# Gated linear attention and a squared-ReLU network on one core: later loads of q, k, v and alpha, pairs of blocks at other places, another order of the opening

## The chip, the cores and the metric

The kernel runs on one core of a Trainium2 chip. The time is that of one execution on the device, in microseconds (us); three executions were timed, and one more was profiled.

## The reference

Four batches, eight heads, 768 steps, head width 48. A state of 48x48 for each head is scaled by alpha and fed by k and v; y is q times the state. The heads of one step side by side are a row x of 384; 3072 such rows go through a network with 2048 hidden units.

```python
for t in range(S):
    state = alpha[:, :, t, :, None] * state + np.einsum('bhd,bhe->bhde', k[:, :, t], v[:, :, t])
    y[:, :, t] = np.einsum('bhd,bhde->bhe', q[:, :, t], state)
...
x = np.ascontiguousarray(attn_out.transpose(0, 2, 1, 3)).reshape(B * S, H * D)
h = np.maximum(x @ w_in, 0.0)
return (h * h @ w_out).astype(np.float32)
```

The inputs and the result stand in DRAM; q, k, v and alpha are float32. The weights arrive as eight-byte floats and are turned into float32 on the chip.

## The kernel before

**Blocks and groups.** A block is 128 steps of one batch with all eight heads; there are 24, numbered so that the four batches of the same steps follow each other. The attention works on pairs of blocks (n, n+1), the network on groups of four blocks (512 rows), six groups. While the network works on group g, the attention makes the x of group g+1, so that TensorE always has products of the network between those of the attention.

**Attention of a block.** `ln` takes the logarithm of alpha (in place, ScalarE), `cs` sums it along the steps (TensorE), `eb` and `ei` take the exponentials of the sums with both signs, `mq` and `mk` multiply q and k by them (VectorE). `qT`, `kT` (for the first blocks) or `turn` (a pair) transpose q and k on TensorE, and `qc`, `kc` copy them from PSUM (ScalarE). `sc` makes the scores, `kv` (state_sums) the sums of k times v, `am` masks the scores, `us` adds the state, `st` makes the next state. `ga` and `gb` are the two halves of a pair's products: each has scores and sums of one new block, and the products y of the pair before. `ya`, `yb` are the y of the first pairs alone. `ev`, in the opening `ep`, copies y from PSUM to x, in four parts; the table `evd` says which copies VectorE takes, the others are ScalarE's. `lt` (lastT) or `bl` and `br` (over DRAM, rows `row` and `last`) bring the last sums of a block to where the state wants them. `zeros` and `warm` are products of zeros, which nobody reads.

**The network.** In group 0 the weights are used in float32 (lines 908 and 798). They come in sixteen parts (`raw`), and each is converted by `first` (VectorE, two operations), `middle` (ScalarE, two) and `second` (VectorE, three). `ha` and `hb` are the first layer's products for the first and second half of group 0's rows, for one slice j of 128 hidden units; each is three matmuls of 256 columns. From group 1 on, and for part of w_out in group 0, each product is made of three passes on parts of the operands: `cast_w`, `rest_w` and `diff_w` split a part of the weights into b, l and d; l and d are stored to DRAM (line 652) and come back part by part (line 683). x is split into xa, xl, xd (`split_x` on ScalarE and VectorE, `diff_x` on VectorE), the hidden values into ha, hl, hd. `in_x` does the first two passes of a slice and `in_y`, two slices later, the third; `out_x` and `out_y` do the same for the second layer. The sums of the output are added on VectorE (`osb`) and stored.

**What sets the order.** The order of each engine is the order of the program. The opening is written out by hand in the string `first`. After it, `weave` goes through a list of the network's units, each with a cost in rows, and puts the attention's events, and those for weights and x, ahead of the first unit that starts at or after their time. The table `AT` holds all those times: `g0`, `g1`, `g` when a pair of blocks starts in group 0, group 1 and later groups; `ga`, `gb` when its two halves come after that; `evs`, `evs0` the distance of the four parts of `ev`; `w_first`, `o0`, `o2`, `wstep`, `w_in_at`, `w_in_by` when the parts of the weights are split; `g0x`, `g1x`, `gx`, `xs` when x is split; `cv0` when the conversions start; `str1` when d of w_out comes back.

**Loads.** All transfers are issued by SyncE, in order; an issue that waits for a buffer holds up those behind it, and each of the eight semaphores of the transfers serves every eighth of them. q, k, v and alpha of a block are four loads of 192 KB. There are two tiles for alpha and for q, three for k, four for v, and a few lent ones in the opening; so a load waits until an earlier block's tile has been read. In `attention`, the next k is asked for with `ga`, two v and one more k with `gb`, two q with `turn`, and alpha with `cs`.

**PSUM.** Eight banks go round among all tiles of TensorE's results; a tile's first product waits until its bank's previous tile was read.

Of the kernel before, what the change touches and what calls it, by code (L numbers as in the profile page):

```python
# [15 lines left out]


GB = 4
AT = {'evs': 0.65, 'lead': 4, 'post': 3, 'w_first': (44.75, 40.75, 51.5), 'wstep': 1.8, 'w_in_at': 2.375, 'w_in_by': 3.4, 'room1': 22, 'room': 24, 's0': 4, 'ahead': 6, 'late': 2, 'xs': 0.2, 'g0': ((0.75, 4, False, True, 25.5), (21.25, 6, True, True), (28.25, 8, True, False)), 'sc0': (2.15, 2.35, 2.35), 'g1': ((5.75, 8, False, 15.5), (15.25, 10, True), (34.5, 12, True)), 'g': ((1.575, 6, True), (15.5, 8, True)), 'g1x': 50.0, 'gx': 46.75, 'g0x': 56.25, 'k0': 2, 'h0': 17, 'k1': 4, 'h1': 0, 'h1by': 2, 'evs0': 0.1, 'tp': 'ADMD', 'tp1': 'ADAD', 'split': 8, 'o0': (46.5, 47.25), 'o1': (), 'o2': (19.75, 27.0, 32.75, 34.0, 42.0, 41.75), 'str1': 24.5, 'ga': 9.5, 'gb': 12.75, 'cv0': 1.125, 'pre': '0a 1a 0q 0k 1k 1q', 'cp': (), 'evd': ((0, 0, 0), (0, 1, 0), (0, 1, 2), (2, 0, 2), (2, 1, 1), (2, 1, 2), (2, 1, 3)), 'first': 'ln0 warm0 ln1 cs0 zeros3 ei0 mk0 eb0 mq0 kT0 cs1 qT0 kc0 eb1 load0v load2a qc0 mq1 sc0 ei1 ln2 qT1 mk1 weights0 qc1 kv0 am0 load1v us0 kT1 kc1 load2k lt1 sc1 kv1 first0 load2q load3a load2v am1 middle0 cs2 eb2 us1 ei2 ya0 yb0 mk2 ln3 mq2 qT2 qc2 cs3 ep00 ep01 load3v load3k ep02 kT2 weights1 kc2 zeros2 load3q second0 lt0 sc2 eb3 kv2 ei3 ep03 zeros3 first1 weights2 middle1 ha0 mq3 mk3 qT3 load4k kT3 qc3 kc3 am2 load4q ha1 second1 sc3 lt2 lt3 st0 kv3 am3 us2 ha2 us3 load4a first2 ya2 yb2 weights3 ep20 ep21 ha3 weights4 ep22 ep23 middle2 st3 hb1 load4v second2 weights5 weights6 st2 hb2 st1 hb3 hb0'}


RUN = {0: 128, 32: 32, 64: 64, 96: 32}
# [3 lines left out]
def kernel(  # L26
# [84 lines left out]
    def load(n, xs="aqkv"):  # L111
        c, b = divmod(n, B)
        for x in xs:
            t = tile_of(x, n)
            if id(t) in owner:
                need(("free", *owner[id(t)]))
            owner[id(t)] = x, n
            given.add((x, n))
            nc.sync.dma_start(  # L119
                out=t[:, :, 0:D] if x in "qk" else t.rearrange("a (h d) -> a h d", h=H),  # L120
                in_=srcs[x][b, :, c * C : (c + 1) * C, :].rearrange("h s d -> s h d"),
            )
# [73 lines left out]

    for word in AT["pre"].split():
        load(int(word[0]), word[1:])
# [53 lines left out]
    def work(name, bufs=1):  # L252
        return p2.tile([128, NP, C], FP32, tag=name, name=name, bufs=bufs)
# [7 lines left out]

    SPLIT = AT["split"]

# [98 lines left out]
    def copied(x, n):  # L362
        t = blk[n][f"{x}s"] = work(f"{x}s", 2 if x == "k" else 4)
        copy = nc.vector.tensor_copy if f"{x}{n}" in AT["cp"] else nc.scalar.copy
        copy(out=t, in_=blk[n].pop(f"{x}T"))
# [219 lines left out]
    def ev(n, ps=tuple(range(NP))):  # L585
# [44 lines left out]
    here, todo, room = {}, [], [22]  # L630
# [8 lines left out]
    late = [False]  # L639
# [20 lines left out]
    def diff_w(w, p):  # L660
# [7 lines left out]
        for x in "ld":  # L668
            t = made.pop((x, w, p))
            if w == "i" or p >= NW - AT["k0"] or (x == "l" and p >= NW - AT["k1"]):  # L670
                here[x, w, p] = t
        pump()

    def prepare(at, w, p):
        step = AT["wstep"]
        fs = (cast_w, rest_w, diff_w)
        return [(at + i * step, f, (w, p)) for i, f in enumerate(fs)]
# [288 lines left out]
    first = AT["first"]  # L966
# [28 lines left out]
    def attention(t, n0, after, scale=1, begun=True, whole_at=None, turn_at=None):  # L995

        out = []
        old = n0 - 2 if after else None
        given = old, n0 if begun and n0 < NBLK else None

        def loads(at, *which):
            out.extend((at, load, (m, x)) for m, x in which if m < NBLK)

        for at, fs in EARLY if n0 < SPLIT else PLAN:
            for f in fs.split():
                w = t + (AT[f] if scale == 1 and f in ("ga", "gb") else at) * scale
                if f in ("ga", "gb") and whole_at is not None:
                    w = whole_at
                if f in ("turn", "kc0", "kc1", "qc0", "qc1", "br0", "br1") and turn_at is not None:
                    w = turn_at + (at - 6.5) * scale  # L1010
                if f == "ga":
                    out.append((w, ga if whole_at is None else joined, given))
                elif f == "gb":
                    if whole_at is None:
                        out.append((w, gb, given))
                    if after:
                        for p in range(NP):
                            out.append((w + AT["evs" if scale == 1 else "evs0"] * p, ev_part, (old, p)))
                if not begun:
                    continue  # L1020
                if f == "ga":
                    loads(w, (n0 + 3, "k"))
                elif f == "gb":
                    loads(w, (n0 + 2, "v"), (n0 + 3, "v"), (n0 + 4, "k"))
                elif n0 >= NBLK:
                    continue
                elif f == "turn":
                    out.append((w, turn, (n0,)))
                    loads(w, (n0 + 2, "q"), (n0 + 3, "q"))
                else:  # L1030
                    n = n0 + int(f[-1])
                    out.append((w, steps[f[:-1]], (n,)))
                    if f[:-1] == "cs":
                        loads(w, (n + 2, "a"))
        return sorted(out, key=lambda x: x[0])

    def weave(units, events, at):
# [55 lines left out]
    cv0 = AT["cv0"]  # L1093
# [10 lines left out]
    for (t, n0, after, run, *other), scale in zip(AT["g0"], AT["sc0"]):  # L1104
        events += attention(t, n0, after, scale, run, *other)
    for g in range(1, NG):
        base.append(begin + sum(u[0] for u in units))
        at0 = base[g]
        units.append((0, begun, (g,)))
        units += layer_in(g) + layer_out(g)  # L1110
        units.append((0, ended, (g,)))
        if g + 1 < NG:
            for t, n0, after, *other in AT["g1"] if g == 1 else AT["g"]:
                n0 = n0 if g == 1 else n0 + GB * g
                other = [None if x is None else at0 + x for x in other]
                events += attention(at0 + t, n0, after, 1, True, *other)
            events += [(at0 + t, f, x) for t, f, x in splits_of_x(AT["g1x" if g == 1 else "gx"], g + 1)]
        if g == 1:
            m = len(AT["w_first"])
            for p in range(m, NW):  # L1120
                events += prepare(at0 + AT["w_in_at"] + AT["w_in_by"] * (p - m), "i", p)
            for i, at in enumerate(AT["o1"] + AT["o2"]):
                events += prepare(at0 + at, "o", order[len(AT["o0"]) + i])
            n = min(AT["k0"], AT["k1"])
            events.append((at0, lambda: todo.extend(("l", "o", p) for p in range(NW - n, NW)), ()))
            events.append((at0 + AT["str1"], stream_out, (AT["k1"], "d")))
        events.append((at0 + 26, stream, (g + 1,)))
# [31 lines left out]
```

## Time and profile before

| what | us |
|---|---|
| median of three runs | 525.36 |
| lowest, highest | 524.78, 529.82 |
| the profiled execution | 526.78 |
| its span, first to last instruction | 525.0 |

The granted clock was 1.000 throughout. The page gives busy time by engine (PE is TensorE's matmuls, PEld its weight loads, DVE is VectorE, ACT ScalarE, POOL GpSimd, SP SyncE), the span in 40 slices with a digit for tenths of busy time, and the chain of work that ended last. "issue" in it is time in which an engine waited for nothing that the profile shows. A wait is written as the waiting engine and line, an arrow, and what ended it, then the total in us, how often, and the longest. A row of the timeline has its start, its length, the engine, the line, the operation and in brackets the idle time before it.

TensorE's busy time is spread so: 4.9 us lie in zeros, 3.8 in warm, 43.3 in the first layer of group 0, 203 in the passes of the first layer later, and 312 in the second layer, of which 54 in float32; the rest is attention.

### The profile page before, as it was taken

What the parts mean: (1) busy time and instruction counts of PE and PEld (TensorE: products, weight loads), DVE (VectorE), ACT (ScalarE), POOL (GpSimd) and SP (SyncE); (2) the same over time, 40 slices, a digit from 0 to 9 for tenths busy, and PEclk for the clock granted to TensorE, in tenths of its full rate; (3) what the DMA queues carried; (4) which work ended last, traced back from release to release, by engine and by line L of the source; (5) the groups of instructions that cost most, each with busy time, mean ns of one, the idle gap of its engine ahead of it and who ended that gap; (6) DMA issues with size and microseconds to landing.
All of it is one profiled execution on the core that took longest, in us unless ns stands there. A gap on an engine that the chain in (4) does not pass through costs nothing.

```text
span 525.0 us, 13021 instructions
## 1 busy us (share of the span) xinstructions
PE 511.3 (97%) x5346; PEld 421.9 (80%) x5346; DVE 362.9 (69%) x627; ACT 305.2 (58%) x650; POOL 5.3 (1%) x29
## 2 busy tenths in 40 slices
PE   8879999999999999999999999999999999999997
PEld 6665455669888669887899987889987899988997
DVE  3677979989879859766596566686464486463861
ACT  5658896575779645475963166953265763164620
POOL 4000000000000000000000000000000000000000
PEclk9999999999999999999999999999999999999999
DMA  9998877555589665998995787855683444699201
GB/s 189 228 248 169 238 162 180 112 153 227 182 221 218 173 192 157 286 305 201 203 263 167 236 234 196 228 162 167 208 282 126 159 151 139 212 373 308 82 2 60
DMA packets 139323, 102.35 MB, mean 195 GB/s; under 512 B 109808, under 2 KB 112896, under 8 KB 139264
## 3 DMA queue, kind: packets, MB, share of 16 engines
q1 hardware_dynamic: 139264, 101.52, 68.6%
q8 instruction: 42, 0.69, 0.5%
q14 instruction: 17, 0.14, 0.1%
HBM read 84.17 MB, written 17.33 MB: 193 GB/s over the span
## 4 chain that ended last, share of the span: by engine, by line
PE 92%; SPq 3%; issue 1%; DMA 1%; ACT 1%; DVE 1%; DVEq 0%; POOLq 0%
PE o L798 41%; PE h L715 31%; PE h L908 7%; PE y L390 4%; SPq L119 3%; PE sckv L410 2%; PE T L567 2%; PE sckv L438 2%; DMA raw<-in_moe_w_in_dram 1%; PE cs L283 1%; PE cs L284 1%; PE cs L280 1%; SPq L136 0%; ACT hid L917 0%; PE lastT L334 0%
## 5 line engine op out<-in xcount | busy, mean ns | idle before, releaser
L715 PE MATMUL h<-xa,wb 128*128 128x512 f32 x240 | 68.8, 395 | 0.0
L715 PE MATMUL h<-xl,wl 128*128 128x512 f32 x240 | 67.8, 391 | 0.9 <-issue 0.9
L715 PE MATMUL h<-xd,wd 128*128 128x512 f32 x240 | 66.7, 393 | 0.1
L605 ACT COPY x<-y 32x256 f32<-32x256 f32 (+3 forms) x134 | 47.9, 365 | 23.2 <-PE y L390 21.0
L637 DVE TENSOR_TENSOR hid<-h,hid 128x512 f32<-128x512 f32 x40 | 27.6, 689 | 46.9 <-PE h L715 46.7
L732 ACT ACTIVATE h<-h 128x512 f32<-128x512 f32 x40 | 23.3, 582 | 62.2 <-PE h L715 62.2
L798 PE MATMUL o<-wb,ha 128*128 128x384 f32 x160 | 54.4, 340 | 1.3 <-issue 1.3
L715 PEld LDWEIGHTS h<-xl,wl 128*128 128x128 f32 x240 | 45.0, 188 | 11.0 <-issue 1.1
L798 PE MATMUL o<-wd,hd 128*128 128x384 f32 x304 | 53.8, 334 | 0.0
L798 PE MATMUL o<-w_out,hid 128*128 128x384 f32 x160 | 53.7, 490 | 0.0
L798 PE MATMUL o<-wl,hl 128*128 128x384 f32 x160 | 53.5, 335 | 0.0
L798 PEld LDWEIGHTS o<-wd,hd 128*128 128x128 f32 x304 | 52.7, 188 | 0.2
L715 PEld LDWEIGHTS h<-xd,wd 128*128 128x128 f32 x240 | 44.5, 188 | 9.7 <-issue 0.5
L715 PEld LDWEIGHTS h<-xa,wb 128*128 128x128 f32 x240 | 44.3, 188 | 9.1
L798 PE MATMUL o<-wb,hx 128*128 128x384 f32 x144 | 48.7, 338 | 0.0
L798 PE MATMUL o<-wl,hx 128*128 128x384 f32 x144 | 48.1, 334 | 0.0
L908 PE MATMUL h<-x,w_in 128*128 128x512 f32 (+1 forms) x120 | 43.3, 510 | 2.9 <-issue 2.0
L798 PEld LDWEIGHTS o<-w_out,hid 128*128 128x128 f32 x160 | 29.9, 190 | 19.9 <-ACT w_out L180 0.2
L730 ACT ACTIVATE hid<-h 128x512 f32<-128x512 f32 x40 | 24.2, 606 | 29.3 <-PE h L715 29.2
L690 ACT ACTIVATE ha<-hid 128x512 fp32r<-128x512 f32 x40 | 25.4, 637 | 25.6 <-DVE hx L642 17.2
L908 PEld LDWEIGHTS h<-x,w_in 128*128 128x128 f32 x120 | 22.3, 190 | 20.4 <-issue 16.9
L642 DVE SCALAR_TENSOR_TENSOR hl<-ha,hid 128x512 fp32r<-128x512 f32 x40 | 27.5, 686 | 12.2 <-ACT ha L690 12.2
(114 smaller groups left out, 869.4 us busy)
## 6 DMA issues: line engine op xcount, KB each, us to landing
wd<-do SPq DMA_DIRECT2D x36, 384.0 KB, 4.9
wl<-lo SPq DMA_DIRECT2D x34, 384.0 KB, 4.4
wl<-li SPq DMA_DIRECT2D x32, 384.0 KB, 4.2
wd<-di SPq DMA_DIRECT2D x32, 384.0 KB, 3.5
raw<-in_moe_w_in_dram SPq DMA_DIRECT2D x8, 768.0 KB
raw<-in_moe_w_out_dram SPq DMA_DIRECT2D x8, 768.0 KB, 4.8
v_in<-in_v_dram SPq DMA_DIRECT2D x24, 192.0 KB, 4.3
out_dram<-osb SPq DMA_DIRECT2D x24, 192.0 KB, 2.4
```

Source lines behind the costliest of these rows:

```text
L119: nc.sync.dma_start(out=t[:, :, 0:D] if x in "qk" else t.rearrange("a (h d) -> a h d", h=H), in_=srcs[x][b, :, c * C : (c + 1) * C, :].rea ...
L390: ins = nc.tensor.matmul(out=ys[e][64 * half : 64 * half + D + G * e, m % 2, p // 2, t], lhsT=lhsT, rhs=rhs, start=(half, e) not in seen, ...
L410: nc.tensor.matmul(out=ps[e][HALF[h], 0, p, :], lhsT=ks[rows, p, HALF[h]], rhs=qs[rows, p, HALF[h]], start=True, stop=True, skip_group_che ...
L605: copy(out=x[kk][to : to + m, t : t + 2], in_=blk[n]["y"][e][r : r + m, :, p // 2],)
L637: nc.vector.tensor_tensor(out=o, in0=x, in1=z, op=op)
L642: nc.vector.scalar_tensor_tensor(out=o, in0=x, scalar=c, in1=y, op0=ALU.mult, op1=op)
L690: nc.scalar.activation(out=a, in_=x, func=AF.Copy, scale=NEAR * E)
L715: nc.tensor.matmul(out=acc["h", j], lhsT=here[w, "i", p][:, kk, jj * 128 : (jj + 1) * 128], rhs=x_parts[x][:, kk], start=start and kk == 0 ...
L730: nc.scalar.activation(out=hid[j], in_=x, func=AF.Copy, scale=E)
L732: nc.scalar.activation(out=x, in_=x, func=AF.Copy, scale=1.0 + E)
L798: nc.tensor.matmul(out=acc[t][:, 0:DM], lhsT=lhs[:, t * C : (t + 1) * C], rhs=rhs, start=start, stop=stop, skip_group_check=True,)
L908: nc.tensor.matmul(out=ps, lhsT=w[:, kk, c0 : c0 + 128], rhs=xT[g][kk][:, cols], start=(kk == 0), stop=(kk == KM - 1),)
```

## The change

`attention` asks for each of its seven loads at a time of its own, by a list `later` of seven numbers, in rows: k of block n0+3 with `ga` as before, v of n0+2 with `gb` as before, v of n0+3 five rows after it, k of n0+4 four rows after it, q of n0+2 with `turn` as before, q of n0+3 one row later, alpha one row after `cs`. In group 0 (scale not 1) nothing is later.

```diff
+        later = AT["later"] if scale == 1 else (0,) * 7
...
                 if f == "ga":
-                    loads(w, (n0 + 3, "k"))
+                    loads(w + later[0], (n0 + 3, "k"))
                 elif f == "gb":
-                    loads(w, (n0 + 2, "v"), (n0 + 3, "v"), (n0 + 4, "k"))
+                    for i, m, x in ((1, n0 + 2, "v"), (2, n0 + 3, "v"), (3, n0 + 4, "k")):
+                        loads(w + later[i], (m, x))
...
                 elif f == "turn":
                     out.append((w, turn, (n0,)))
-                    loads(w, (n0 + 2, "q"), (n0 + 3, "q"))
+                    loads(w + later[4], (n0 + 2, "q"))
+                    loads(w + later[5], (n0 + 3, "q"))
...
                     if f[:-1] == "cs":
-                        loads(w, (n + 2, "a"))
+                        loads(w + later[6], (n + 2, "a"))
```

The table `AT` is one line of the file; these are the entries of it that change, one to a line:

```diff
+'later': (0, 0, 5, 4, 0, 1, 1)
-'evs': 0.65, 'evs0': 0.1
+'evs': 0.5, 'evs0': 0.5
-'w_first': (44.75, 40.75, 51.5), 'wstep': 1.8, 'w_in_at': 2.375, 'w_in_by': 3.4
+'w_first': (46.75, 40.5, 50.75), 'wstep': 1.4, 'w_in_at': 2.25, 'w_in_by': 3.6
-'xs': 0.2, 'g1x': 50.0, 'gx': 46.75, 'g0x': 56.25
+'xs': 0.05, 'g1x': 52.0, 'gx': 48.25, 'g0x': 55.75
-'g0': ((0.75, ...), (21.25, ...), (28.25, ...)), 'sc0': (2.15, 2.35, 2.35)
+'g0': ((-0.25, ...), (22.25, ...), (28.25, ...)), 'sc0': (2.45, 2.35, 2.35)
-'g1': ((5.75, 8, False, 15.5), (15.25, 10, True), (34.5, 12, True))
+'g1': ((4.5, 8, False, 16.25), (14.25, 10, True), (34.75, 12, True))
-'g': ((1.575, 6, True), (15.5, 8, True))
+'g': ((2.075, 6, True), (14.25, 8, True))
-'o0': (46.5, 47.25), 'o2': (19.75, 27.0, 32.75, 34.0, 42.0, 41.75), 'str1': 24.5
+'o0': (47.5, 46.75), 'o2': (22.0, 26.25, 25.25, 38.5, 39.75, 35.0), 'str1': 19.5
-'ga': 9.5, 'gb': 12.75, 'cv0': 1.125, 'pre': '0a 1a 0q 0k 1k 1q'
+'ga': 9.75, 'gb': 12.5, 'cv0': 0.875, 'pre': '0a 1a 0q 0k 1q 1k'
-'evd': ((0, 0, 0), (0, 1, 0), (0, 1, 2), (2, 0, 2), (2, 1, 1), (2, 1, 2), (2, 1, 3))
+'evd': ((0, 1, 0), (0, 1, 2), (2, 0, 2), (2, 1, 0), (2, 1, 1), (2, 1, 2), (2, 1, 3))
```

The opening's order (`first`), the same steps but for zeros2, which is gone:

```diff
-ln0 warm0 ln1 cs0 zeros3 ei0 mk0 eb0 mq0 kT0 cs1 qT0 kc0 eb1 load0v load2a qc0 mq1 sc0 ei1 ln2 qT1 mk1 weights0 qc1 kv0 am0 load1v us0 kT1 kc1 load2k lt1 sc1 kv1 first0 load2q load3a load2v am1 middle0 cs2 eb2 us1 ei2 ya0 yb0 mk2 ln3 mq2 qT2 qc2 cs3 ep00 ep01 load3v load3k ep02 kT2 weights1 kc2 zeros2 load3q second0 lt0 sc2 eb3 kv2 ei3 ep03 zeros3 first1 weights2 middle1 ha0 mq3 mk3 qT3 load4k kT3 qc3 kc3 am2 load4q ha1 second1 sc3 lt2 lt3 st0 kv3 am3 us2 ha2 us3 load4a first2 ya2 yb2 weights3 ep20 ep21 ha3 weights4 ep22 ep23 middle2 st3 hb1 load4v second2 weights5 weights6 st2 hb2 st1 hb3 hb0
+ln0 warm0 ln1 cs0 zeros3 ei0 mk0 eb0 mq0 kT0 cs1 load2a qT0 kc0 load0v eb1 qc0 sc0 mq1 ei1 ln2 weights0 qT1 am0 qc1 kv0 mk1 load1v first0 kT1 us0 kc1 lt1 sc1 load2q load2k kv1 load3a am1 cs2 eb2 us1 ei2 middle0 ya0 yb0 load2v mk2 ln3 mq2 qT2 qc2 kT2 load3k cs3 ep00 ep01 load3q ep02 load3v kc2 lt0 weights1 sc2 eb3 kv2 second0 ei3 ep03 zeros3 first1 weights2 lt2 middle1 ha0 load4q mk3 mq3 qT3 am2 kT3 qc3 kc3 ha1 sc3 lt3 st0 kv3 load4k second1 am3 us2 ha2 us3 load4a ya2 first2 yb2 weights5 ep20 ep21 weights3 ha3 weights6 ep22 ep23 weights4 middle2 second2 st3 st2 hb2 st1 load4v hb3 hb0 hb1
```

More of the change, by code (lines that the diff above doesn't have):

```diff
@@ L18 @@
 GB = 4
-AT = {'evs': 0.65, 'lead': 4, 'post': 3, 'w_first': (44.75, 40.75, 51.5), 'wstep': 1.8, 'w_in_at': 2.375, 'w_in_by': 3.4, 'room1': 22, 'room': 24, 's0': 4, 'ahead': 6, 'late': 2, 'xs': 0.2, 'g0': ((0.75, 4, False, True, 25.5), (21.25, 6, True, True), (28.25, 8, True, False)), 'sc0': (2.15, 2.35, 2.35), 'g1': ((5.75, 8, False, 15.5), (15.25, 10, True), (34.5, 12, True)), 'g': ((1.575, 6, True), (15.5, 8, True)), 'g1x': 50.0, 'gx': 46.75, 'g0x': 56.25, 'k0': 2, 'h0': 17, 'k1': 4, 'h1': 0, 'h1by': 2, 'evs0': 0.1, 'tp': 'ADMD', 'tp1': 'ADAD', 'split': 8, 'o0': (46.5, 47.25), 'o1': (), 'o2': (19.75, 27.0, 32.75, 34.0, 42.0, 41.75), 'str1': 24.5, 'ga': 9.5, 'gb': 12.75, 'cv0': 1.125, 'pre': '0a 1a 0q 0k 1k 1q', 'cp': (), 'evd': ((0, 0, 0), (0, 1, 0), (0, 1, 2), (2, 0, 2), (2, 1, 1), (2, 1, 2), (2, 1, 3)), 'first': 'ln0 warm0 ln1 cs0 zeros3 ei0 mk0 eb0 mq0 kT0 cs1 qT0 kc0 eb1 load0v load2a qc0 mq1 sc0 ei1 ln2 qT1 mk1 weights0 qc1 kv0 am0 load1v us0 kT1 kc1 load2k lt1 sc1 kv1 first0 load2q load3a load2v am1 middle0 cs2 eb2 us1 ei2 ya0 yb0 mk2 ln3 mq2 qT2 qc2 cs3 ep00 ep01 load3v load3k ep02 kT2 weights1 kc2 zeros2 load3q second0 lt0 sc2 eb3 kv2 ei3 ep03 zeros3 first1 weights2 middle1 ha0 mq3 mk3 qT3 load4k kT3 qc3 kc3 am2 load4q ha1 second1 sc3 lt2 lt3 st0 kv3 am3 us2 ha2 us3 load4a first2 ya2 yb2 weights3 ep20 ep21 ha3 weights4 ep22 ep23 middle2 st3 hb1 load4v second2 weights5 weights6 st2 hb2 st1 hb3 hb0'}
@@ new lines @@
+AT = {'later': (0, 0, 5, 4, 0, 1, 1), 'evs': 0.5, 'lead': 4, 'post': 3, 'w_first': (46.75, 40.5, 50.75), 'wstep': 1.4, 'w_in_at': 2.25, 'w_in_by': 3.6, 'room1': 22, 'room': 24, 's0': 4, 'ahead': 6, 'late': 2, 'xs': 0.05, 'g0': ((-0.25, 4, False, True, 25.5), (22.25, 6, True, True), (28.25, 8, True, False)), 'sc0': (2.45, 2.35, 2.35), 'g1': ((4.5, 8, False, 16.25), (14.25, 10, True), (34.75, 12, True)), 'g': ((2.075, 6, True), (14.25, 8, True)), 'g1x': 52.0, 'gx': 48.25, 'g0x': 55.75, 'k0': 2, 'h0': 17, 'k1': 4, 'h1': 0, 'h1by': 2, 'evs0': 0.5, 'tp': 'ADMD', 'tp1': 'ADAD', 'split': 8, 'o0': (47.5, 46.75), 'o1': (), 'o2': (22.0, 26.25, 25.25, 38.5, 39.75, 35.0), 'str1': 19.5, 'ga': 9.75, 'gb': 12.5, 'cv0': 0.875, 'pre': '0a 1a 0q 0k 1q 1k', 'cp': (), 'evd': ((0, 1, 0), (0, 1, 2), (2, 0, 2), (2, 1, 0), (2, 1, 1), (2, 1, 2), (2, 1, 3)), 'first': 'ln0 warm0 ln1 cs0 zeros3 ei0 mk0 eb0 mq0 kT0 cs1 load2a qT0 kc0 load0v eb1 qc0 sc0 mq1 ei1 ln2 weights0 qT1 am0 qc1 kv0 mk1 load1v first0 kT1 us0 kc1 lt1 sc1 load2q load2k kv1 load3a am1 cs2 eb2 us1 ei2 middle0 ya0 yb0 load2v mk2 ln3 mq2 qT2 qc2 kT2 load3k cs3 ep00 ep01 load3q ep02 load3v kc2 lt0 weights1 sc2 eb3 kv2 second0 ei3 ep03 zeros3 first1 weights2 lt2 middle1 ha0 load4q mk3 mq3 qT3 am2 kT3 qc3 kc3 ha1 sc3 lt3 st0 kv3 load4k second1 am3 us2 ha2 us3 load4a ya2 first2 yb2 weights5 ep20 ep21 weights3 ha3 weights6 ep22 ep23 weights4 middle2 second2 st3 st2 hb2 st1 load4v hb3 hb0 hb1'}
```

## The prediction

> **What bounds the kernel now.** First the busy times and the DMA queues of the page, to see which engine has no room.
>
> ```profile
> PE 511.3 (97%) x5346; PEld 421.9 (80%) x5346; DVE 362.9 (69%) x627; ACT 305.2 (58%) x650; POOL 5.3 (1%) x29
> PE   8879999999999999999999999999999999999997
> DMA  9998877555589665998995787855683444699201
> q8 instruction: 42, 0.69, 0.5%
> ```
>
> TensorE is busy in 97% of the span; only the first three slices and the last show less than a 9. A change that only reorders can therefore win no more than TensorE's idle time (13.7 us of 525.0) plus fillers. So the second view is what TensorE waits for, and the third the chain in order of time, which puts a place to each wait.
>
> ```profile
> PE h L908 <- issue: 2.0, 1, 2.0
> PE y L390 <- issue: 1.7, 3, 0.7
> PE o L798 <- issue: 1.3, 1, 1.3
> PE h L715 <- issue: 0.9, 1, 0.9
> PE h L908 <- ACT x L605: 0.8, 1, 0.8
> SPq L119 <- PE y L390: 20.6, 7, 6.7
> ...
> 36.19 2.04 issue
> 240.34 0.89 issue
> 317.43 0.62 issue
> 343.83 1.27 issue
> 399.10 0.37 issue
> 521.60 0.56 DVE osb L637
> ```
>
> Nearly all of TensorE's waits are "issue": no semaphore ends them. I counted its records (weight loads, matmuls, waiting instructions) in order of start. The six issue waits stand before records 449, 1217, 5569, 7361, 8129 and 9153: their distances are 768, 4352, 1792, 768 and 1024, all multiples of 256. The instruction queue brought 42 packets of 16,384 bytes, and 10,836 records over 42 are 258. So I read them as TensorE waiting for its next 256 instructions. In the five after the first the packet started 2.2 to 2.6 us before the wait ended, e.g. at 238.64 for the one ending at 241.23.
>
> A block of 256 lasts long in dense matmuls and about 2 us in a burst of small attention products. The wait comes where a block is shorter than the packet's delay plus those 2.5 us. The delay varied: the packet started 3.18 us after the block's beginning at 235.46, with the DMA share of those microseconds near 0.9 to 1.3, and 0.20 after 396.83, with DMA idle.
>
> The opening has one place where two waits stack:
>
> ```profile
> 38.23 1.24 PE L908 MATMUL h<-x,w_in 128*128 128x256 f32 x5 [2.04 <-issue]
> 40.30 5.01 PE L908 MATMUL h<-x,w_in 128*128 128x256 f32 x21 [0.84 <-ACT x L605]
> 38.64 0.38 ACT L914 ACTIVATE r<-h 128x256 f32<-128x256 f32 x1 [1.76 <-PE h L908]
> 39.49 0.75 ACT L605 COPY x<-y 32x256 f32<-32x256 f32 x2
> ```
>
> Record 1217 is the last matmul of ha3. ScalarE's relu of ha3 stands ahead of the last two copies of x, so all of it slides, and the second halves (hb) start late.
>
> **The change part by part.** After 41 us TensorE computes the same products. zeros2 goes (3 matmuls, 12 records), 13 waiting instructions come: 10,837 records for 10,836. What can change is waits alone, against this execution: 526.78 us, span 525.0, 1.78 around it. The median of the runs, 525.36, is 1.42 lower; I carry the difference over.
>
> *Opening.* zeros2 (the row at 20.56, 1.46 us) is filler: what follows waits for x and w_in, so it costs and brings nothing. The second part of w_in is issued behind one more 192 KB load (q of block 3, v of block 3 also reordered): at 222 GB/s of the window 25 to 30 that is 0.87 us, so its conversion starts at 26.05, not 25.18. mk3 now precedes mq3 (0.55): qT3 about 28.2 for 26.88. Back come half of the lastT products (0.89/2), moved into idle time ahead. On VectorE: first1 1.03, mk3 and mq3 1.11, am2 0.67, st0 0.83, second1 2.73, to 32.4; am3 and the sums 1.29, to 33.7. So y starts near 33.9 for 32.92, 1.0 late, and ha3 ends at 37.3. But the new order puts the block's end (record 1217) 8 records inside hb2, behind ha3. ScalarE's relu and square (0.38 + 0.42) then run at 37.4 to 38.2, VectorE's seven copies (five took 2.11) end near 38.9, and the last two of ScalarE (0.75), which wait for some of them, near 39.4. The packet: before, 7.23 us from block's beginning (31.00) to the wait's end (38.23); from 31.9 that gives 39.1. So the work that resumed at 40.30 resumes at 39.4: **-0.9**. Ends: -2.1 if w_in lands as before; +0.9 if packet and copies stack again (39.2 + 2.04 = 41.2).
>
> *One v and one k later, q and a one row later.* SyncE is in order; loads waiting for y held 20.6 us of its queue (7 times), and weight streams stood behind them. But TensorE lost 0.2 us in all to a weight stream, so the relief itself is hidden: 0. Deadlines: v of the odd block is now issued 5 rows after gb, 7.2 rows before its use; one row is about 1.3 us (1.08 rows are 8 matmuls of 174.5 ns), so 9.3 us against a median landing of 4.3: no cost. The cover is 5 us; past it each microsecond would stall TensorE. It works at the waits: around 235 us one q load of 192 KB leaves the crowd, 0.7 us at 271 GB/s.
>
> *Pairs closer* moves blocks against the bursts. By nominal spacings (228 ns for h, about 15 ns for burst records) the block ahead of 5569 shrinks from 4.53 to 4.11 us: +0.4 for a packet 0.7 earlier, **-0.3** (ends -0.9, +0.4). The one ahead of 8129 grows from 2.66 to 3.94, since two xd products (6 x 0.228) come in: the wait of 1.27 leaves about 0.2, **-1.1** (ends -1.27, 0). The one ahead of 7361 stays at 1.93: 0. The one ahead of 9153 begins 16 records earlier, at the burst's first record: **-0.2** (ends -0.37, 0).
>
> *New waits.* In the second group of blocks' first turn an h product takes a PSUM bank 1.30 us after the last transpose into it (nearest before: 3.35, no wait). ScalarE has an h to scale first (0.60 from the turn's start), then three copies (two took 0.64): done near 1.6, needed at 1.88. **+0.1** (ends 0, +1.3 with one more such op ahead). x of the third group is split 2 rows (2.6 us) later: xl ended at 214.7, first use 217.77; with one output sum (0.6) now between, xl ends near 217.9, its last use at 218.2: **+0.2** (ends 0, +1.0). evs 0.65 to 0.5 and the other starts of cast and rest of w: ScalarE idles 62 us before one line, VectorE 47, both for h of TensorE: 0; their cover gone, a copy costs 0.37.
>
> Sum: -0.9 - 0.3 - 1.1 - 0.2 + 0.1 + 0.2 = **-2.2**: 524.6 for the profiled execution, **523.2** for the median. All ends together give -4.6 to +3.6: 520.7 to 529.0.
>
> [...]
>
> **The rivals.** *The waits do not follow the blocks.* Then only the opening's order counts, and 5569, 8129 and 9153 keep theirs: -0.9 + 0.4 = -0.5, 524.9. For: the delay differs by 3 us from block to block for reasons I read only partly. Against: six distances in multiples of 256.
>
> *Slower: a packet misses the burst near 76 us.* Before, that block began 9 records ahead of the burst, in matmuls of 429 ns, and the packet came 2.40 us before it. Now it begins 6 records inside, and lasts 2.4 us. Ready 2.5 us after its start, the packet costs nothing while it starts within -0.1 us of the block's beginning; shifted by the 15 records I expect -1.0. If it starts 3.2 us late as at 235, TensorE loses 3.2: -2.2 + 3.2 = +1.0, 526.4; with the opening stacked again (+1.8), 528.2. DMA was light there, which speaks against.
>
> *Much faster: the thinner DMA queue lets every packet come in time.* Then 0.89 + 0.62 + 1.27 + 0.37 and the opening's 2.0 + 0.8 + 0.7 go: -6.7, less the slower chain of 1.0: -5.7, 519.7. Against: at 396 us DMA was idle and there was a wait.
>
> **How the numbers follow.** Forecast 0.50; waits not following 0.20; slower 0.15; much faster 0.13; else 0.02. The likeliest gives 523.2. Range 519.8 to 527.5: it takes in the first two, most of the fast rival and half of the slow one. 1% is 5.25 us, about what a measurement of this kernel can tell from no change (the three runs span 5.0). Faster by that (under 520.1) needs the fast rival: 0.11. Slower (over 530.6) needs the slow one and the upper ends together: 0.06. Within: 0.83.
>
> **What would show it.** The issue waits again at distances of 256; none at record 8129 above 0.3, one of 0.6 at 7361; hb's steady run starting near 39; no wait at the first burst near 75; no wait over 0.5 at the first h of the third group. A TensorE wait for v, k or a weight stream would make the prediction wrong, and so would y of the opening ending after 37.

## The result and the profile after

The changed kernel took 522.8 us in the median of 14 runs (521.7 to 523.84); the kernel before, on the same chip, 525.95. One of the 14 runs of the kernel before took 847.25 us, a slow run that the ratio leaves out. The ratio is 0.9919, with a 95% interval of 0.9899 to 0.9939. The profiled execution took 523.38 us with a span of 521.6; before it was 526.78 and 525.0. So the time fell by 3.15 us in the medians and by 3.4 in the profiled executions: within 1%, and nearly half as much again as the forecast of 2.2.

From the page of the changed kernel, first busy time, share and instructions, then the granted clock in 40 slices, then a DMA queue with packets, MB and share:

```profile
PE 511.3 (98%) x5340; PEld 422.0 (81%) x5340; DVE 363.7 (70%) x628; ACT 304.8 (58%) x649; POOL 5.3 (1%) x29
PEclk9899999999999999999999999999999999999999
q8 instruction: 42, 0.69, 0.6%
```

TensorE's busy time is the same 511.3 us; only its waits shrank. (The busy times by part that stand ahead of the prediction add up to more than 511.3, because the passes of a layer overlap and each was counted by itself. Counted as one, the first layer's later passes are busy for 170.7 us and the second layer for 215.1.) The granted clock has an 8 in the second slice, which it had not before. What TensorE waited for (total, times, longest):

```profile
PE sckv L410 <- ACT ks L365: 2.0, 3, 1.4
...
PE h L908 <- DVE x L605: 0.8, 1, 0.8
...
PE h L715 <- issue: 0.5, 1, 0.5
...
PE y L390 <- issue: 0.2, 1, 0.2
```

And the waits that the chain holds (start, length, what):

```profile
17.62 0.22 issue
...
240.83 0.51 issue
...
518.17 0.56 DVE osb L637
```

Of the five issue waits that the prediction shows, the one at 36.19 (2.04 us), the one at 317.43 (0.62), the one at 343.83 (1.27) and the one at 399.10 (0.37) are gone; 0.89 has become 0.51. Where that shows in time, by the start of the first product of each group's first layer, and of the first `cs` after `hb`:

| point | before | after | difference | stretch's share |
|---|---|---|---|---|
| first `cs` after the opening | 47.30 | 47.44 | +0.14 | +0.14 |
| group 1 | 129.44 | 129.60 | +0.16 | +0.02 |
| group 2 | 217.09 | 217.14 | +0.05 | -0.11 |
| group 3 | 297.92 | 297.45 | -0.47 | -0.52 |
| group 4 | 379.45 | 376.71 | -2.74 | -2.27 |
| group 5 | 455.34 | 451.91 | -3.43 | -0.69 |
| last output sum | 521.60 | 518.17 | -3.43 | 0.00 |

The three stretches that gained are those with the waits of 0.89, of 0.62 and 1.27, and of 0.37. They gained a little more than the idle times, because the first products after a wait also start slower: by their spacing from start to start the waits of before (0.89, 0.62, 1.27 and 0.37) cost 1.06, 0.82, 1.43 and 0.57 us.

The opening won nothing, although its stacked pair of waits went. The timeline of the changed kernel (start, length, engine, line, operation, shapes, count, idle time before):

```profile
22.97 0.78 PE L410 MATMUL sckv<-qs,ks 48*64 48x64 f32 x32 [1.44 <-ACT ks L365]
...
24.51 2.71 PE L378 MATMUL zeros<-s 128*128 128x256 f32 x6
...
39.66 7.94 PE L908 MATMUL h<-x,w_in 128*128 128x256 f32 x28 [0.80 <-DVE x L605]
...
26.84 0.56 DVE L163 TENSOR_SCALAR power<-raw 128x768 uint32<-128x768 uint32 x1 [2.06 <-DMA raw<-in_moe_w_in_dram]
```

and two rows of the kernel before:

```profile
40.30 7.16 PE L908 MATMUL h<-x,w_in 128*128 128x256 f32 x26 [0.84 <-ACT x L605]
...
25.18 0.56 DVE L163 TENSOR_SCALAR power<-raw 128x768 uint32<-128x768 uint32 x1 [1.02 <-DMA raw<-in_moe_w_in_dram]
```

In the changed kernel VectorE stands 2.06 us for the second part of w_in, which it has at 26.84 (before: 25.18). And six products of zeros take 2.71 us. The windows (from and to, then length, busy time of PE, PEld, DVE, ACT and POOL, the granted clock, the DMA share, GB/s) say why:

```profile
22.00:24.00 2.00, 1.03 (x52) 1.03 (x56) 1.97 (x4) 1.94 (x6) 0.00 (x0) 0.86 0.52 90
24.00:26.00 2.00, 2.00 (x28) 1.64 (x21) 0.79 (x1) 1.13 (x4) 0.00 (x0) 0.50 0.98 334
26.00:28.00 2.00, 2.00 (x22) 1.44 (x21) 1.16 (x3) 0.27 (x2) 0.00 (x0) 0.79 1.04 387
```

After the idle 1.44 us, where zeros2 stood before, the granted clock fell to 0.50. The last y began at 36.64 us (before 34.69). The first layer's products resumed at 39.66, 0.64 us earlier than before, but with 28 of them left ahead of the first `cs` and not 26, and they took 7.94 us for 7.16.

### The profile page after: what moved, and what is told of

It is laid out like the page before. It is cut to its first block, busy times and chain, and to the rows that moved or that the text cites. A ratio compares the mean times of both kernels' runs of the same rounds, so it can differ in the third digit from the quotient of the medians.

```text
span 521.6 us, 13021 instructions
## 1 busy us (share of the span) xinstructions
PE 511.3 (98%) x5340; PEld 422.0 (81%) x5340; DVE 363.7 (70%) x628; ACT 304.8 (58%) x649; POOL 5.3 (1%) x29
## 4 chain that ended last, share of the span: by engine, by line
PE 94%; SPq 2%; ACT 1%; DMA 1%; DVE 1%; issue 0%; POOLq 0%; DVEq 0%
PE o L798 41%; PE h L715 32%; PE h L908 7%; PE y L390 5%; PE sckv L410 2%; PE T L567 2%; PE sckv L438 2%; SPq L119 1%; DMA v_in<-in_v_dram 1%; PE cs L280 1%; PE cs L283 1%; PE cs L284 1%; PE zeros L378 1%; DVE x L605 0%; ACT x L605 0%
## 5 line engine op out<-in xcount | busy, mean ns | idle before, releaser
L715 PE MATMUL h<-xd,wd 128*128 128x512 f32 x240 | 68.4, 397 | 0.5 <-issue 0.5
L605 ACT COPY x<-y 16x256 f32<-16x256 f32 (+2 forms) x133 | 46.9, 365 | 22.6 <-PE y L390 18.8
L690 ACT ACTIVATE ha<-hid 128x512 fp32r<-128x512 f32 x40 | 25.5, 640 | 15.7 <-PE o L798 9.0
L637 DVE TENSOR_TENSOR osb<-o,osb 128x384 f32<-128x384 f32 x24 | 12.9, 556 | 26.6 <-PE o L798 25.4
```

The costliest lines, as they stand in the source:

```text
L605: copy(out=x[kk][to : to + m, t : t + 2], in_=blk[n]["y"][e][r : r + m, :, p // 2],)
L637: nc.vector.tensor_tensor(out=o, in0=x, in1=z, op=op)
L690: nc.scalar.activation(out=a, in_=x, func=AF.Copy, scale=NEAR * E)
L715: nc.tensor.matmul(out=acc["h", j], lhsT=here[w, "i", p][:, kk, jj * 128 : (jj + 1) * 128], rhs=x_parts[x][:, kk], start=start and kk == 0 ...
```

## The experiments

Block here means 256 instruction records of TensorE, as the prediction reads them from the places of the six waits and from 42 instruction packets for 10,836 records, not a block of steps, unless it is said; the expectations say "chunk" for a block of steps. Every ratio is to the kernel before, on the same chip.

**Do the waits belong to blocks of records? (shift72)** The kernel before, with its third group of zeros made of other products:

```diff
+        calls.append(n)
+        if len(calls) == 3:
+            for _ in range(21):
+                nc.tensor.matmul(
+                    out=ps[0:48, 0, 0:1], lhsT=s_t[3].rearrange("a p d -> a (p d)")[:, 0:48],
+                    rhs=s_t[3][:, 0, 0:1], start=True, stop=True, skip_group_check=True,
+                )
+            return
```

> The kernel before with its third group of zeros made of 21 products of one column in place of three of 256 (the zeros are filler; 72 records more ahead of everything after it, no place and no load changed). Theory A (a wait belongs to a block of records): all later ends of blocks come 72 records earlier in the work; no block of under 2 us ends at the turns of the 3rd and 4th group any more, so the waits of 0.62 near 318, 1.27 near 345 and 0.37 near 399 us go (-2.0 to -2.3 us), and new ones of 0.3 to 1.0 may stand where blocks of 1.9 us now end, near 237 and 263 us: span 522.5 to 524 if the opening is as long as it was. Theory B (the waits belong to the place in the work, to the turn of a group, and not to the block): 0.62, 1.27 and 0.37 stay within 0.3 us, span 524.5 to 526.

Measured: ratio 1.0024 (0.9988 to 1.0061), median 528.41, span 527.5. Its chain:

```profile
35.53 1.50 issue
...
237.73 3.16 issue
...
267.14 0.83 issue
...
524.13 0.56 DVE osb L647
```

The waits of 0.62, 1.27 and 0.37 are gone, with no place and no load changed, and new ones stand at the ends of two of the blocks that are now short, near 238 and 267 us (237 and 263 were expected). So the waits belong to the blocks, and theory B falls. The size of the new one was missed: 3.16 for 0.3 to 1.0; and so was the span, 527.5 for 522.5 to 524. During the long wait the granted clock began to fall: 0.70, 0.50 and 0.95 in the three windows from 240 to 246 us. From the first `cs` after the opening (48.37 for 47.30) to the last output sum it took 475.76 us, for 474.30 before.

**What starts a packet? (turn_earlier)** The kernel before, with the turn a place earlier:

```diff
-        (6.5, "turn br1"),
-        (7.0, "kc0 qc0 kc1 qc1 br0"),
+        (5.5, "turn br1"),
+        (6.0, "kc0 qc0 kc1 qc1 br0"),
```

> The kernel before with the turn of each pair one place earlier in the plan (5.5 for 6.5, the copies of k and q 6.0 for 7.0), one h product between turn and scores more, ends of blocks where they were to within one record. Theory A (the packet for the block after next is asked for when TensorE's sequencer gets past an end of a block, and the scores' wait for ScalarE's copies of q and k holds the sequencer in front of it): copies come about 1.4 to 2.8 us earlier against the scores, packets near 315.8 and 397.0 start 1.4 us or more earlier relative to their block's start, the waits of 0.62 and 0.37 go, and 1.27 near 345 falls below 0.5: span 523 to 524. Theory B (only the length of the block in time counts): blocks are as short as before, the waits stay within 0.3 us, span 524.5 to 526.

Measured: ratio 1.0088 (1.0059 to 1.0118), span 529.4. The three waits went, as theory A said; the span did not fall to the 523 to 524 expected, because the turn now comes before its inputs. The groups of TensorE's waits:

```profile
PE T L567 <- DVE q_in L299: 2.9, 4, 0.9
PE h L908 <- issue: 1.6, 1, 1.6
PE sckv L410 <- DVE us L451: 1.2, 1, 1.2
...
PE o L798 <- DMA wd<-do: 1.1, 1, 1.1
```

No issue wait over 0.3 us is left after the opening; four transposes wait for VectorE's multiplication of q instead. Blocks were as short as before (1.8 us at records 7105 to 7361), so the length alone does not decide. What does, at the two turns with blocks of about 2 us, in four kernels (us; packet is the start of the instruction packet at that turn):

| kernel, turn | ScalarE's last copy of q ends | packet starts | first scores | packet against scores | wait |
|---|---|---|---|---|---|
| before, group 3 | 315.42 | 315.81 | 315.19 | +0.62 | 0.62 |
| changed, group 3 | 313.64 | 313.64 | 316.08 | -2.44 | 0 |
| turn_earlier, group 3 | 317.95 | 318.99 | 321.07 | -2.08 | 0 |
| no_zeros2, group 3 | 313.52 | 314.27 | 313.29 | +0.98 | 1.12 |
| before, group 4 | 396.95 | 397.03 | 396.72 | +0.31 | 0.37 |
| changed, group 4 | 392.91 | 392.85 | 395.35 | -2.50 | 0 |
| turn_earlier, group 4 | 398.73 | 400.33 | 401.85 | -1.52 | 0 |
| no_zeros2, group 4 | 394.13 | 394.15 | 393.90 | +0.25 | 0.45 |

In no row does the packet start more than 0.06 us before the copies are done, and in five of eight it starts within 0.4 us of that. Among the scores' weight loads are some that wait for these copies (before, at the turn of group 3, the loads that start at 315.19 us have 0.35 us of idle time ahead of them, ended by ScalarE's qs), so the reading is that TensorE's sequencer stands at them and that a packet starts only behind that. Moving the copies moved the packets, which bears it out for these two turns. It is not the whole rule. In the eight further profiles of the kernels below, of sixteen such packets fourteen start no more than 0.1 us before the copies end, but at the turn of group 4 one starts 0.39 us before (after_again) and one 1.35 us before (only_places, 393.35 against 394.70). In these two the end of the block lies ahead of the scores, by one record and by ten, as it does in five cases where the packet has no such lead. And it is not shown that nothing else holds a packet.

ScalarE's rows of the kernel before say why its copies were late there:

```profile
312.62 0.58 ACT L732 ACTIVATE h<-h 128x512 f32<-128x512 f32 x1 [1.89 <-PE h L715]
...
314.69 0.73 ACT L575 COPY qs<-T 128x256 f32<-128x256 f32 x2
```

and those of the changed kernel:

```profile
310.69 0.58 ACT L732 ACTIVATE h<-h 128x512 f32<-128x512 f32 x1 [0.43 <-PE h L715]
...
312.92 0.72 ACT L575 COPY qs<-T 128x256 f32<-128x256 f32 x2
```

From the first transpose to the first scores it is 5.5 us in both, with eighteen products between. But before, ScalarE had first to wait 1.89 us for an h that stood ahead of the copies in its queue; with the pair at its new place that h is done when the transposes come. The copies start 0.75 us after the transposes' first product (310.58) in place of 3.41 (309.70).

**Only the places (only_places).** The kernel before, with the pairs of blocks at their new places and nothing else of the change:

```diff
-'g': ((1.575, 6, True), (15.5, 8, True)), 'ga': 9.5, 'gb': 12.75
+'g': ((2.075, 6, True), (14.25, 8, True)), 'ga': 9.75, 'gb': 12.5
```

> The kernel before with three entries alone changed: `g`, `ga` and `gb`, the places of the pairs of blocks; loads, opening and all other times as before. Theory A: the packets at the first burst of groups 3 to 5 start before the burst, since the copies of q and k end over 2 us ahead of it; the waits of 0.62, 1.27 and 0.37 go, span 522.6 to 523.4 (-1.6 to -2.4), ratio 0.995 to 0.997. Rival B: the loads are together as before, so the waits stay, span 524.5 to 525.5, ratio 0.999 to 1.001. The opening stays as it was (2.04 and 0.84).

Measured: ratio 0.9964 (0.9936 to 0.9991), span 523.4. The waits of 0.62, 1.27 and 0.37 are gone, so these three entries alone remove them. The span came as theory A had it, in part by luck: 1.0 of the 1.6 us lies in the opening, which is that of before and was expected to stay, but whose two waits were 0.63 and 0.60 in this profile. From the first `cs` (46.30) to the last output sum (519.96) it took 473.66 us, against 474.30 before and 470.73 in the changed kernel. By stretches, the two with the turns gained 1.61 and 0.69 us against before, and the one from group 2 to group 3 lost 1.49. New small waits took part of that: two of TensorE for ScalarE's work on x (0.39 and 0.40), 0.36 for wd from DRAM, 0.43 of issue. The changed kernel has none of the first three, so other entries of the change, perhaps those for x and for the parts of the weights, bring the rest; which of them does it was not tried.

**Only the later loads taken out (loads_together).** The changed kernel with all seven delays at zero:

```diff
-'later': (0, 0, 5, 4, 0, 1, 1)
+'later': (0, 0, 0, 0, 0, 0, 0)
```

> The changed kernel with all seven numbers of `later` at 0: q, k, v and alpha are asked for together again, everything else as changed. Theory A (the gain is the instruction waits, and those went because TensorE's sequencer gets past its semaphore waits earlier, which is set by the places of the pairs): no issue wait after 41 us over 0.9, span within 0.5 us of the changed kernel's 521.6, ratio to before 0.990 to 0.994. Rival B (the thinner DMA queue let the packets come in time): issue waits of 0.5 or more come back at records near 7361, 8129 and 9153, 2 to 3 us in all, span 523.5 to 524.6, ratio 0.996 to 0.999.

Measured: ratio 0.9929 (0.9902 to 0.9957), median 522.8 like the changed kernel's, span 520.7, which is 0.9 below the changed kernel's where 0.5 was allowed. Most of the difference lies in the opening: from group 1 on no stretch between the points of the table above differs by more than 0.15 us from the changed kernel's. The later loads bring nothing that can be measured. They do act: with the loads together, VectorE waits again for the row that comes back over DRAM, as it did before and does not in the changed kernel. First the row of the kernel before, then that of loads_together:

```profile
241.78 0.36 DVE L468 TENSOR_TENSOR s<-s,last 128x192 f32<-128x192 f32 x1 [2.80 <-DMA last<-row]
...
240.26 0.36 DVE L468 TENSOR_TENSOR s<-s,last 128x192 f32<-128x192 f32 x1 [2.51 <-DMA last<-row]
```

TensorE waits 0.62 us for VectorE at 242.74, and has no issue wait near 241 in that profile; but after_again, with the later loads, has none there either.

**zeros2 put back (zeros_back).**

```diff
-... lt0 weights1 sc2 eb3 ...
+... lt0 weights1 zeros2 sc2 eb3 ...
```

> The changed kernel with zeros2 put back ahead of the scores of block 2, where TensorE waits 1.44 us in the changed kernel; 12 records more, so every end of a block of 256 records lies 12 records earlier in the work. Two questions. Clock: if the fall of the granted clock to 0.50 at 24 to 26 us came from that wait, it is 1.00 there now and zeros3 takes 1.5 us, not 2.7; first cs after hb 0.2 to 0.6 earlier than 47.44. Blocks: by nominal spacings the block ahead of record 5569 lasts 2.80 us, not 4.11, so its wait grows from 0.51 to 1.4 to 2.0 us; if the waits do not follow the blocks it stays at 0.5. Span 521.6 - 0.4 + 1.2 = 522.4 by the first, 521.2 by the second.

Measured: ratio 0.9955 (0.9927 to 0.9982), span 522.6, clock 1.00 throughout. Twelve records more move the block's end back into the products before `hb`, and the stacked pair returns:

```profile
39.03 1.56 PE L908 MATMUL h<-x,w_in 128*128 128x256 f32 x6 [1.74 <-issue]
41.43 2.86 PE L908 MATMUL h<-x,w_in 128*128 128x256 f32 x12 [0.84 <-ACT x L605]
```

The first group starts at 48.43 for 47.44. From there to the last output sum it takes 470.73 us, to the hundredth as in the changed kernel. So a filler that nobody reads is worth a microsecond here by where it puts a block's end, although the clock was better; the first of the two expectations, a start 0.2 to 0.6 us earlier, was missed. The wait before record 5569 stayed at 0.50, which the expectation had put down for waits that do not follow the blocks. The trace says otherwise: the block's end cuts the work twelve records earlier, as it should, and the block ahead of it lasts 2.77 us (2.80 expected, 4.05 in the changed kernel); but its packet started 1.07 us after the block's beginning, not 2.66. The size of a wait needs both, and the expectation had held the packet fixed.

**zeros2 taken out of before (no_zeros2).**

```diff
-... weights1 kc2 zeros2 load3q second0 ...
+... weights1 kc2 load3q second0 ...
```

> The kernel before with zeros2 alone left out of its order of the opening (12 instruction records of TensorE fewer ahead of the third chunk's scores; the zeros that it made were filler). Theory A (the waits at a block of 256 records follow what the block's end cuts and how early TensorE's sequencer gets past it): the end of the opening's block moves behind the h product that it cut, so before's stacked pair at 38.2 and 41 us (2.04 + 0.84 us) goes; further back every block end moves 12 records later, the short blocks at 7361 and 9153 stay short and keep their waits within 0.3 us of 0.62 and 0.37, and the one at 8129 gets a block of about 3.8 us and falls from 1.27 to under 0.5. Together -1 to -3 us; the granted clock falls below 0.9 between 22 and 28 us as it did in the changed kernel, which gives up to 1.3 us of it back. Theory B (before's opening waits were a chance of that one profile, and zeros2 holds the clock up): 0 to +1.5 us, and the waits further back stay as they were, 1.27 among them.

Measured: ratio 0.9966 (0.9935 to 0.9997), span 522.3; the profile is 2.7 us shorter, the median 1.3. The pair in the opening went (first group at 45.91 for 47.30), and so did 1.27. The waits of the chain after the opening:

```profile
315.62 1.12 issue
...
396.38 0.45 issue
...
518.85 0.56 DVE osb L637
```

The 0.62 became 1.12, outside the 0.3 given; 0.89 near 241 vanished, and a wait of 0.51 for wd from DRAM stands at 225.57. The clock fell to 0.50 between 24 and 26 us, as theory A had it.

**The order of the opening (opening_before, opening_before_again, opening_before_third).** The changed kernel with the entries `pre`, `evd` and `first` of before, zeros2 left out:

```diff
-'pre': '0a 1a 0q 0k 1q 1k', 'evd': ((0, 1, 0), ..., (2, 1, 0), ...)
+'pre': '0a 1a 0q 0k 1k 1q', 'evd': ((0, 0, 0), (0, 1, 0), ...)
```

> The changed kernel with the opening's order, first loads and the share of the copies of before, but without zeros2, so that TensorE's records keep their numbers to within three. Theory A: the opening gave nothing (first cs after hb at 47.30 before, 47.44 changed), so the time is that of the changed kernel: span 521.2 to 522.2. Rival C: the new order of the opening earns what its DMA order and its fallen clock cost, and without it the opening is over 0.5 us worse or better than in both kernels: first cs after hb before 46.8 or after 48.0.

> The changed kernel with the order of the opening of before, without zeros2 (the kernel of the run opening_before once more). If the changed order of the opening costs time, as the starts of the first group said (46.05 against 47.44 us), this kernel's ratio to before lies at 0.987 to 0.990, below the changed kernel's interval's middle of 0.992, and its span at 520.0 to 521.2. If the earlier run's 46.05 was the scatter of one profile, the ratio is 0.991 to 0.993 and the span 521.3 to 522.

> The changed kernel with the order of the opening of before, without zeros2, on the same chip as the changed kernel. If its two earlier ratios (0.989, 0.988) hold, it lies 0.2 to 0.5% below the changed kernel, with the first group at 45.2 to 46.1 us; if they were scatter, within 0.1% of it.

> The changed kernel once more, as the measure for its neighbours in this job: ratio 0.990 to 0.994, one issue wait of 0.3 to 0.6 near 241 us and none over 0.4 at the turns of the 3rd and 4th group, first group at 46.7 to 47.5 us.

Measured: ratios 0.989 (0.984 to 0.994), 0.9882 (0.9845 to 0.992) and 0.9885 (0.9855 to 0.9915), medians 521.67, 520.69 and 520.85. The changed kernel beside the third (after_again): 0.9915 (0.9887 to 0.9944), median 522.18 (521.58 to 523.37, against 520.43 to 521.81). The first group starts at 46.05, 45.24 and 46.02 with the old order, at 47.44, 46.85 and 46.72 with the new one (changed kernel, after_again, loads_together). So the new order costs about 1.2 us, as rival C of the first expectation allowed and theory A did not, and the old one without zeros2 makes the fastest kernel here. The issue wait that was expected near 241 in after_again did not come. Of the second of these profiles, among TensorE's waits:

```profile
PE h L908 <- DVE x L605: 0.3, 1, 0.3
PE h L908 <- ACT x L605: 0.3, 1, 0.3
PE h L715 <- issue: 0.2, 1, 0.2
```

The intervals of the ratios overlap with the changed kernel's; that three of three lie below it, and the trace's 1.2 us, carry the finding. The first of the three profiles has an issue wait that the two others have not: 0.62 us at 322.15, where the block after the one at 7361 ends. Its packet started 3.07 us after that block began, for 2.45 and 1.10 in the two others. So the same kernel can have or lack such a wait from one profile to the next.

**Is the late part of w_in the cause? (w_earlier)**

```diff
-... cs3 ep00 ep01 load3q ep02 load3v kc2 lt0 weights1 sc2 ...
+... cs3 ep00 ep01 weights1 load3q ep02 load3v kc2 lt0 sc2 ...
```

> The changed kernel with the second part of w_in asked for ahead of q and v of the fourth chunk in its opening (two 192 KB loads behind it instead of in front of it; nothing else). Theory A (the changed order of the opening is late because VectorE stands waiting for this part at 26.84 us, 2.06 us of idle, with the casts of the third chunk's q and k queued behind it): asked for some 1.6 us earlier it lands at 24.8 to 25.5, the casts, the transposes that wait for them and the y products come about as much earlier, the last y starts at 34.5 to 35.5 instead of 36.64 and 35.91, and the first group's first product after hb starts at 45.2 to 46.2 instead of 47.44 and 46.72: ratio to before 0.988 to 0.990. Theory B (the order of TensorE's own steps costs the time): last y at 35.9 or later, first group at 46.7 or later, ratio 0.991 to 0.993. A wait for q or v of the fourth chunk in their place would show as a TensorE or VectorE wait for them near 27 to 31 us.

Measured: ratio 0.9911 (0.9881 to 0.9941), median 521.92, beside 522.18 of after_again. What the expectation calls casts are the multiplications mk3 and mq3. Its profile:

```profile
24.34 0.55 DVE L163 TENSOR_SCALAR power<-raw 128x768 uint32<-128x768 uint32 x1
...
23.96 2.91 PE L378 MATMUL zeros<-s 128*128 128x256 f32 x6
...
28.66 0.60 PE L351 MATMUL qT<-ident,qk_lent 128*128 128x128 f32 x4
```

and that of after_again:

```profile
26.46 0.56 DVE L163 TENSOR_SCALAR power<-raw 128x768 uint32<-128x768 uint32 x1 [2.19 <-DMA raw<-in_moe_w_in_dram]
...
23.55 1.56 PE L378 MATMUL zeros<-s 128*128 128x256 f32 x6
...
28.49 0.66 PE L351 MATMUL qT<-ident,qk_lent 128*128 128x128 f32 x4 [1.43 <-DVE qk_lent L299]
```

VectorE's conversion of the part starts 2.1 us earlier (24.34, ahead of the 24.8 to 25.5 of theory A), and its wait is gone. Yet qT comes at the same time. In after_again, with the full clock, TensorE waits 1.43 us for VectorE; in w_earlier the clock fell (0.83, 0.50 and 0.82 in the three windows from 22 to 28 us), TensorE itself was late by as much, and waited for nothing. Two delays of the same length lie side by side, and taking one away shows only when the other is absent. The last y (36.32) and the first group (47.12) are theory B's numbers, but that TensorE's order is the rest of the cause is only argued.

## Why the prediction was right, and where not

| step of the sum | forecast | measured |
|---|---|---|
| opening | -0.9 | +0.14 |
| block ahead of 5569 | -0.3 | -0.38 (0.89 to 0.51) |
| block ahead of 8129 | -1.1 | -1.27 (gone) |
| block ahead of 7361 | 0 | -0.62 (gone) |
| block ahead of 9153 | -0.2 | -0.37 (gone) |
| wait for a PSUM bank | +0.1 | 0 |
| x of the third group | +0.2 | 0 |

The measured waits add to -2.64 us; the slower restart after the three that are gone (0.16 to 0.20 us each) and the opening make it -3.1 of the -3.4 between the profiled executions. That the forecast of -2.2 came within 1.2 us of this is partly luck: the opening was forecast 1.0 too good, and the rest 2.2 too small. The whole came out nearly right; the split did not. A small slip stands in the first rival, too: its +0.4 is not derived, and the two new waits give +0.3. And the range was said to take in most of the fast rival, whose own time, 519.7, lies just outside it.

*The blocks.* The reading of the issue waits as waits for the next 256 records held; shift72 shows it by moving the blocks alone. Ahead of 8129 the block grew as forecast (2.76 to 4.03 us), but by the forecast that alone would have left about 0.2; the packet, too, came earlier, 0.59 us after the block's beginning for 1.89. In turn_earlier that wait is gone with the block at 2.92 us and the packet at 0.13. In the changed kernel the chain shows a wait at two of 42 packets, 0.22 and 0.51 us; in shift72 one wait alone is 3.16 us.

*Ahead of 7361 and 9153.* "Stays at 1.93: 0" is the step that failed. It took the packet's start against the block's as given, and counted only the block's length. At both turns ScalarE's copies came 2.7 us earlier against the scores (their end from 0.23 us after the first scores to 2.44 before), and the packet with them: at the turn of group 3 from 0.62 after to 2.44 before. That was worth the whole of both waits.

*The opening.* The waits went as forecast: the block's end lies behind ha3 and 2.04 + 0.84 us of stacked waits became 0.80. The products resumed at 39.66 for the forecast 39.4, so that step was nearly right: -0.64 for -0.9. What failed is the step from there to the end. The forecast took the work left at the resumption as the same, but two products more were left, and the start was slower: 7.78 us to the first `cs` for 7.00 before, a term that the sum put at nothing. The part of w_in also came 1.66 us later, not 0.87 (1.15 and 1.28 in loads_together and after_again), and the last y ended at 36.86, for about 35.9 by the forecast (1.0 later than the 34.91 of before), close to the 37 that was named as the mark of a wrong prediction. All this is one profile against one: three profiles with the opening of before give 46.30 to 47.30 for the first `cs`, three with the new one 46.72 to 47.44. And "zeros2 is filler, it costs and brings nothing" was wrong both ways. Taken out of before's order alone, the first group starts at 45.91, and with the change's other entries at 45.24 to 46.05, against 46.30 to 47.30 in three profiles with zeros2 in that order (48.37 in shift72, with its 72 records more). But without it the granted clock fell to 0.50 between 20 and 28 us in four of eight profiles, with it in none of five.

*The zeros.* Later loads: 0, as the ratios of 0.9919 and 0.9929 and the stretches show. The two new waits: neither appeared; why not was not followed up. TensorE's wait for v, named as a mark of a wrong prediction, is 0.59 us at 15.22, but it was 0.54 before.

*The rivals.* That the waits do not follow the blocks is out: shift72 moved their places, and zeros_back shows that their sizes follow the packet as well as the block's length. The packet that misses the burst near 76 us: no wait there in any of these kernels. The thinner DMA queue: the waits at the turns are as absent with the loads together, and in only_places too, which has all the loads of before.

*Left open.* The wait near 241 us. Its packet starts 0.7 to 3.0 us after its block begins in eight profiles of the changed kernel and its variants, and the wait is 0 to 0.93. So the -0.38 of one profile, close to the forecast, lies within that scatter. At the same place shift72's is held 2.4 us past ScalarE's last copy, so the copies are not what holds it there.

## What to carry to other kernels

In this kernel the issue waits moved with the count of TensorE's records, in blocks of 256: 72 records more ahead of them took away the waits of 0.62, 1.27 and 0.37 us and put new ones of 3.16 and 0.83 elsewhere (shift72), 12 fewer took away the 2.04 and 0.84 of the opening and the 1.27 (no_zeros2). Where a trace shows such waits, what an edit far away does to the time must be looked for there. At two turns of this kernel 22 of 24 packets started no more than 0.1 us before ScalarE's copies, for which some of the next weight loads wait, were done; where a trace shows the same, bring the producer of these waits ahead in its own queue before counting on a longer block. Before a filler is called free, look at the idle time that it fills: zeros2 went with both the clock and the place of a block, with opposite signs (without it the clock fell to 0.50 near 25 us in four of eight profiles, with it in none of five; taken out of before's order, it moved the first group from 47.30 to 45.91 us).

## What the runs showed of the hardware

All eight profiles without zeros2 have an idle stretch of TensorE of 1.1 to 1.44 us that ends between 21.9 and 23.4 us. In four of the eight the granted clock then fell to 0.50; in the five with zeros2 it did not fall there. In each of the four the clock then missing sums to 1.7 us over the windows from 22 to 28 us ((0.14 + 0.50 + 0.21) x 2 in the changed kernel), as much as 3.4 us at 0.50. In the changed kernel the mean over the window from 23.45 to 26.86 us is 0.50. So a fall followed idle time of this length in four of eight profiles, and idle time alone does not decide: the kernel before, with its stacked waits of 2.04 and 0.84 us, has TensorE busy for 1.42 of the 4 us from 36 to 40, and its clock is 1.00 there. And the clock fell in two profiles at another place as well, with zeros2 in the order or not: in shift72 and opening_before_third, near 16 us (0.63 and 0.57 in the window from 16 to 20).
